# Narrow pieces of the output product in triples instead of pairs, on one core

## The chip, the cores and the metric

The kernel runs on one core of a Trainium2 chip. Its time is the device time of one launch in microseconds, the median of several runs. It computes with five engines: TensorE (PE, with its weight loads as PEld), VectorE (DVE), ScalarE (ACT), GpSimd (POOL) and SyncE (SP), which issues the DMAs.

## What is computed

Attention over chunks of 32 rows with some context and memory rows, then two feed-forward blocks on its 3072 rows of 512 columns. The change lies in the last one:

```python
x = attention(q, k, v, mem_k, mem_v)              # 3072 x 512
h = x @ moe_w_in                                  # 512 x 2048
x = (relu(h) + log1p(exp(-abs(h)))) @ moe_w_out
out = ((x @ moe2_w_a) * (x @ moe2_w_b)) @ moe2_w_out    # 512 x 1536, 1536 x 512
```

## The kernel before

Every float is split into a high and a low fp32r part, and a product is made of three matmuls: high x high, high x low, low x high. The stage of the change is the last block. Its 3072 tokens are worked in `NPAIR` = 3 pairs of two blocks of 512 tokens, and in each pair over `NF2` = 12 steps f of 128 of the 1536 inner columns. A step computes a and b of both token blocks by seven wide products of Winograd's kind instead of eight (`product`, L808, six matmuls of 512 columns each, recorded at L815): 11, s2, s3, s1, 12, 22, s4, in that order, into the PSUM tiles pX, pY, pW, pV, pX, pW, pV. VectorE adds them up behind each (`tt`, L949 to L991) into q and r, which are the products a*b of the two token blocks.

Two steps, even and odd, are a group m (`GROUP` = 2). In the second and third pair, all groups but the very last (11 in all) are worked by `block_step` (L936), and their output product too is of Winograd's kind: from q and r of both steps the operands a11, s3 (even step) and s1, s2, a22, a12, s4 (odd step) are made by VectorE and GpSimd, split by ScalarE (`hi_of`, recorded at L921) and VectorE or GpSimd (`lo_of`, L925). A product of them with the weights `w2o` and `tw` is done in 14 pieces in the next group's two steps, in the order `TURNS` (L867). A piece is called by its product and half here:

1.0 1.1 5.0 6.0 6.1 3.0 7.0 7.1 5.1 4.0 4.1 3.1 2.0 2.1

A piece (`block_product`, L872) is six narrow matmuls of 256 columns (L888) into a PSUM bank, and an addition of the bank to the output tile y by VectorE (L899; a copy by ScalarE, L897, where it is the first). Products 1, 6, 7, 4 and 2 use bank `acc1` for half 0 and `acc2` for half 1; 5 and 3 use `acc3`. Each bank exists once, so a piece waits until the addition of the piece before it on that bank has read it. In a pair's last group the finished y is stored from there (L902).

Where the pieces stand is said by `next_blocks(f, k)` (L909), called seven times a step, behind each wide product: k = 0 behind 11, 1 behind s2, 2 behind s3, 3 behind s1, 4 behind 12, 5 behind 22, 6 behind s4. In the code of a step this is

```python
        at(5)
        next_job()
        next_blocks(f, 5)
        if odd:
            ...                                   # s1 (L983), s2 (L986), their high halves
        product(v, p, f, "s4", False)
        tt(q, v, q, ALU.add)                      # L990
        tt(q, x, q, ALU.mult)                     # L991
        if odd:
            lo_of(p, m, "s1", s1, V)
            lo_of(p, m, "s2", s2, G)
            ...
        at(6)
        next_blocks(f, 6)
```

All engines work in the order in which the program issues (`manual_schedule`, L1190). `at(k)` (L1244) issues the fetches of the weights of the next step (`fetch_u` L800, `fetch_o` L804, `fetch_t` L796), and in step 11 of the second pair and step 0 of the third the splits of the third pair's operands (`split_hi`, `split_lo`, L665). The last group of the third pair is worked by `pair_step` (L1013), which calls `next_blocks` in the same places; in its odd step one piece stands at k = 5 and none at k = 6, and the last one comes behind all steps (L1325).

Of the kernel before, what the change touches and what calls it, by code (L numbers as in the profile page):

```python
# [47 lines left out]
GROUP = 2  # L48
# [3 lines left out]
def attn_moe_moe2(ctx: ExitStack, tc: tile.TileContext, q, k, v, mem_k, mem_v,  # L52
# [851 lines left out]
    def next_job(blocks=False):  # L904
        if jobs and (len(jobs[0]) == 5) == blocks:
            p, m, *which = jobs.pop(0)[:4]
            (block_product if blocks else job)(p, m, *which)

    def next_blocks(f, k):  # L909
        if (f + k) % GROUP == 0:  # L910
            next_job(True)
            next_job(True)

    due = {}
# [21 lines left out]
    def block_step(p, f, at):  # L936
# [6 lines left out]
        nc.scalar.copy(q, x)  # L943
        at(0)
        next_blocks(f, 0)
        late_due(0)
        y = bank("att", f"pY{p}_{f}")
# [5 lines left out]
        at(1)  # L953
        next_job()
        next_blocks(f, 1)
        w = bank("att", f"pW{p}_{f}")
        product(w, p, f, "s3", True)
        r = temp("r", f"r{p}_{f}")
        tt(r, w, q, ALU.add)
        at(2)  # L960
        next_job()
        next_blocks(f, 2)
        late_due(2)
        v = bank("acc0", f"pV{p}_{f}")
# [403 lines left out]
```

## Time and profile before

| | |
|---|---|
| median of 3 runs | 1160.2 us (1159.97 to 1160.5) |
| the profiled execution | 1160.61 us, of which the span of instructions 1158.8 |
| TensorE (PE) busy | 1149.9 us, 99% of the span |
| weight loads (PEld) | 1009.2 us, 87% |
| VectorE (DVE) | 820.7 us, 71% |
| ScalarE (ACT) | 542.0 us, 47% |
| GpSimd (POOL) | 354.3 us, 31% |

How to read it: shares are of the whole span, so they mix stages. An engine off the path may be busy or idle at no cost; what counts is what the bounding engine stands for. Names such as pz (narrow pieces), pX to pV (wide products), y, gh, e, d, s, o_s, o_a are the program's tiles.

### The profile page before, as it was taken

To read this page: it belongs to the slowest core of one execution; us is meant where nothing else is said; L and a number is where in the kernel's file an instruction comes from. 1 tells how busy PE (TensorE), PEld (TensorE's weight loads), DVE (VectorE), ACT (ScalarE), POOL (GpSimd) and SP (SyncE) were. 2 spreads that over 40 slices of the span, in tenths; PEclk is the share of its full clock that TensorE was granted. 3 is DMA by queue.
4 is the path that set the end of the run, shared out by engine and by line. 5 is a ranking of instruction groups with operands and counts; after the bars stand their busy time and mean duration, and the time that the engine had idled before them with its cause. 6 is when DMAs were issued, how large, how long until landed. Compare 5 with 4: busy or idle time off the path is not lost.

```text
span 1158.8 us, 20590 instructions
## 1 busy us (share of the span) xinstructions
PE 1149.9 (99%) x7474; PEld 1009.2 (87%) x7474; DVE 820.7 (71%) x1700; ACT 542.0 (47%) x1233; POOL 354.3 (31%) x296
## 2 busy tenths in 40 slices
PE   9999999999999999999999999999999999999998
PEld 7899999999998888888888888888888888888887
DVE  6889668767677657652376777988667779667776
ACT  6899666665665665554654433232321123221120
POOL 2000323232232223222313565811323544323330
PEclk9999999999999999999999999999999999999999
DMA  8964264454454353321734668672975553975521
GB/s 226 274 227 101 68 142 125 119 132 97 101 130 115 80 132 103 96 68 56 236 134 165 255 254 311 251 273 104 364 273 203 182 200 110 342 279 197 198 84 73
DMA packets 199061, 199.32 MB, mean 172 GB/s; under 512 B 123648, under 2 KB 152240, under 8 KB 198960
## 3 DMA queue, kind: packets, MB, share of 16 engines
q1 hardware_dynamic: 198576, 197.96, 53.6%
q8 instruction: 59, 0.97, 0.3%
q14 instruction: 42, 0.34, 0.1%
q0 software_dynamic: 384, 0.05, 0.0%
HBM read 141.33 MB, written 56.62 MB: 171 GB/s over the span
## 4 chain that ended last, share of the span: by engine, by line
PE 91%; ACT 3%; DVE 3%; DMA 1%; issue 1%; SPq 1%; DVEq 0%; ACTq 0%
PE px L594 21%; PE ph L561 21%; PE pz L888 10%; PE pW L815 9%; PE pV L815 8%; PE pX L815 8%; PE py L850 6%; PE pY L815 4%; PE pxa L482 2%; PE sc L437 1%; DMA kp<-in_k_dram 1%; DVE tmp L126 1%; ACT sm L387 1%; DVE w L134 0%; ACT work L387 0%
## 5 line engine op out<-in xcount | busy, mean ns | idle before, releaser
L561 PE MATMUL ph<-x,w 128*128 128x384 f32 (+1 forms) x1344 | 285.4, 360 | 0.1
L594 PE MATMUL px<-gh,w 128*128 128x384 f32 (+1 forms) x896 | 266.8, 358 | 0.0
L561 PEld LDWEIGHTS ph<-x,w 128*128 128x128 f32 x1344 | 240.6, 188 | 24.8 <-ACT x L373 0.2
L573 DVE SCALAR_TENSOR_TENSOR e<-ph,e 128x384 f32<-128x384 f32 (+1 forms) x112 | 68.7, 614 | 161.0 <-ACT e L572 160.5
L594 PEld LDWEIGHTS px<-gh,w 128*128 128x128 f32 x896 | 165.5, 188 | 15.7 <-DVE e L607 0.3
L594 PE MATMUL px<-gl,w 128*128 128x384 f32 (+1 forms) x448 | 160.3, 358 | 0.0
L582 POOL TENSOR_TENSOR gl<-e,gh 128x384 fp32r<-128x384 f32 (+1 forms) x80 | 94.9, 1187 | 178.9 <-ACT gh L579 178.8
L899 DVE TENSOR_TENSOR y<-pz,y 128x512 f32<-128x512 f32 x138 | 91.1, 683 | 17.6 <-PE pz L888 14.7
L570 ACT ACTIVATE e<-ph 128x384 f32<-128x384 f32 (+1 forms) x112 | 59.5, 531 | 90.4 <-PE ph L561 71.6
L579 ACT CAST gh<-e 128x384 fp32r<-128x384 f32 (+1 forms) x112 | 62.6, 559 | 79.4 <-DVE e L573 59.8
L594 PEld LDWEIGHTS px<-gl,w 128*128 128x128 f32 x448 | 84.1, 188 | 7.6
L925 POOL TENSOR_TENSOR o_s<-s,o_s 128x512 fp32r<-128x512 f32 x33 | 43.4, 1314 | 147.0 <-ACT o_s L921 144.5
L921 ACT CAST o_s<-s 128x512 fp32r<-128x512 f32 x44 | 27.4, 622 | 125.3 <-DVE s L983 92.6
L850 PE MATMUL py<-w2o,c 128*128 128x512 f32 (+1 forms) x342 | 84.8, 386 | 0.1
L454 DVE STREAM_TRANSPOSE af<-sm 32x256 f32<-32x256 f32 x180 | 78.2, 434 | 2.6
L850 PEld LDWEIGHTS py<-w2o,c 128*128 128x128 f32 x342 | 63.4, 188 | 13.9 <-DVE c L1070 0.8
L387 ACT ACTIVATE sm<-sm,st 128x96 f32<-128x96 f32 x168 | 60.6, 362 | 19.2 <-DVE st L383 19.2
L572 ACT ACTIVATE e<-e 128x384 f32<-128x384 f32 (+1 forms) x112 | 64.0, 571 | 3.5
L571 ACT ACTIVATE e<-e 128x384 f32<-128x384 f32 (+1 forms) x112 | 64.0, 571 | 3.5
L921 ACT CAST o_a<-e 128x512 fp32r<-128x512 f32 x22 | 13.7, 621 | 96.6 <-DVE e L991 81.6
L394 POOL TENSOR_TENSOR sm<-sm,st 128x768 f32<-128x768 f32 x18 | 26.5, 1473 | 103.2 <-DVE st L392 103.2
L888 PEld LDWEIGHTS pz<-tw,o_s 128*128 128x128 f32 x396 | 53.4, 190 | 3.7
(191 smaller groups left out, 2130.4 us busy)
## 6 DMA issues: line engine op xcount, KB each, us to landing
u<-u_scratch SPq DMA_DIRECT2D x72, 512.0 KB
u_scratch<-u SPq DMA_DIRECT2D x36, 512.0 KB
w2o<-w2o_scratch SPq DMA_DIRECT2D x24, 512.0 KB
tw<-t_scratch SPq DMA_DIRECT2D x22, 512.0 KB
raw<-in_moe_w_in_dram SPq DMA_DIRECT2D x16, 512.0 KB
raw<-in_moe_w_out_dram SPq DMA_DIRECT2D x16, 512.0 KB
vn<-in_v_dram SPq DMA_DIRECT2D x35, 176.0 KB
raw_a<-in_moe_w_a_dram SPq DMA_DIRECT2D x12, 512.0 KB
```

The lines of the kernel that those rows point to most:

```text
L387: nc.scalar.activation(sm[:, h], sm[:, h], AF.Exp, bias=st[:, 0, h:h + 1], scale=-1.0, accum_out=st[:, 1, h:h + 1])
L454: nc.vector.transpose(out=af[32 * kb:32 * kb + 32, x], in_=self.sm[32 * x:32 * x + 32, :, 32 * kb:32 * kb + 32])
L561: nc.tensor.matmul(ph, lhsT=w[:, a, kt * P:(kt + 1) * P], rhs=x[:, c, kt, :], start=n == 0, stop=n == 3 * KT - 1)
L571: nc.scalar.activation(e, e, AF.Exp, scale=-1.0)
L572: nc.scalar.activation(e, e, AF.Ln, bias=1.0)
L573: nc.vector.scalar_tensor_tensor(e, ph, 0.0, e, ALU.max, ALU.add)
L582: engine.tensor_tensor(lo, e, hi.bitcast(F32), ALU.subtract)
L594: nc.tensor.matmul(acc[t][i][:, :WIDTHS[t]], lhsT=a, rhs=c, start=f == 0 and m == 0, stop=f == NF1 - 1 and m == 2)
L815: nc.tensor.matmul(bank[:, :T2], lhsT=u[:, j, a, kt * P:kt * P + P], rhs=x[kt][:, c], start=first_ and m == 0, stop=m == 3 * KH - 1, skip_ ...
L850: nc.tensor.matmul(b, lhsT=c[:, x, r], rhs=w[:, y, cols], start=n == 0, stop=n == 3 * GROUP - 1)
L888: nc.tensor.matmul(b[:, j], lhsT=c[:, x, r], rhs=w(y), start=begin and i == j == 0, stop=i == 2, skip_group_check=True)
L899: tt(y, b, y, ALU.add)
```

## The change

`next_blocks` no longer issues two pieces wherever f + k is even, but a number given by a table over the step's parity and k. The order of the pieces stays.

```diff
     def next_blocks(f, k):
-        if (f + k) % GROUP == 0:
-            next_job(True)
+        for _ in range({(0, 1): 3, (0, 4): 3, (1, 0): 3, (1, 3): 3, (1, 6): 2}.get((f % GROUP, k), 0)):
             next_job(True)
```

Before, the pairs stand at k = 0, 2, 4, 6 of the even step and 1, 3, 5 of the odd one: seven places a group. After it, triples stand at k = 1 and 4 of the even and 0 and 3 of the odd step, and a pair (2.0, 2.1) at k = 6 of the odd one: five places.

## Rows read from the trace of the kernel before

**Rows 1.** The page, part 1: busy us (share of the span) and instructions of each engine

```profile
PE 1149.9 (99%) x7474; PEld 1009.2 (87%) x7474; DVE 820.7 (71%) x1700; ACT 542.0 (47%) x1233; POOL 354.3 (31%) x296
```

**Rows 2.** Busy time by stretches: us, busy of each engine, granted clock, DMA share, GB/s

```profile
968.00:998.00 30.00, 29.83 (x166) 25.29 (x165) 26.54 (x37) 7.14 (x11) 12.94 (x8) 1.00 0.41 130
```

**Rows 3.** Timeline of TensorE: start us, us, engine, line, out<-in, count

```profile
905.63 1.59 PE L888 MATMUL pz<-w2o,o_a 128*128 128x256 f32 x12
907.06 1.55 PE L815 MATMUL pV<-xb,u 128*128 128x512 f32 x6
908.45 1.52 PE L815 MATMUL pX<-x,u 128*128 128x512 f32 x6
909.81 1.59 PE L888 MATMUL pz<-w2o,o_a 128*128 128x256 f32 x12
```

**Rows 4.** Timeline of VectorE, the end of an odd step

```profile
905.83 0.69 DVE L975 TENSOR_TENSOR d<-pW,e 128x512 f32<-128x512 f32 x1 [2.06 <-PE pW L815]
906.56 0.69 DVE L976 TENSOR_TENSOR gh<-d,gh 128x512 f32<-128x512 f32 x1
907.17 1.28 DVE L899 TENSOR_TENSOR y<-pz,y 128x512 f32<-128x512 f32 x2
908.37 0.68 DVE L983 TENSOR_TENSOR s<-gh 128x512 f32<-128x512 f32 x1
909.15 0.69 DVE L986 TENSOR_TENSOR s<-s,e 128x512 f32<-128x512 f32 x1
909.76 0.68 DVE L990 TENSOR_TENSOR e<-pV,e 128x512 f32<-128x512 f32 x1
...
911.09 1.33 DVE L925 TENSOR_TENSOR o_s<-s,o_s 128x512 fp32r<-128x512 f32 x1
912.34 1.27 DVE L899 TENSOR_TENSOR y<-pz,y 128x512 f32<-128x512 f32 x2
```

**Rows 5.** Waits from 815 us on: waiter, releaser, us in total, times, longest

```profile
PEld pz L888 <- DVE y L899: 0.4, 1, 0.4
```

**Rows 6.** Timelines of TensorE and VectorE, where the second pair ends

```profile
967.10 1.52 PE L815 MATMUL pX<-x,u 128*128 128x512 f32 x6
968.56 1.69 PE L888 MATMUL pz<-w2o,o_a 128*128 128x256 f32 x12
970.09 1.55 PE L815 MATMUL pY<-xs,u 128*128 128x512 f32 x6
...
967.82 1.28 DVE L899 TENSOR_TENSOR y<-pz,y 128x512 f32<-128x512 f32 x2
```

**Rows 7.** The chain of waits (start, us, what), and splits in VectorE's timeline

```profile
964.31 1.57 PE pz L888 x12
...
973.00 1.77 PE pz L888 x12
...
976.16 1.36 PE pX L815 x6
979.62 1.39 PE pW L815 x6
981.01 1.63 PE pV L815 x6
...
957.27 2.31 DVE L665 TENSOR_TENSOR x<-x,x 128x1024 fp32r<-128x1024 f32 x1
...
966.69 1.22 DVE L665 TENSOR_TENSOR xa<-xs,xa 128x1024 fp32r<-128x1024 f32 x1
```

**Rows 8.** Timelines of GpSimd and VectorE: the subtractions of low halves

```profile
910.58 1.29 POOL L925 TENSOR_TENSOR o_s<-s,o_s 128x512 fp32r<-128x512 f32 x1 [11.91 <-ACT o_s L921]
...
956.67 0.68 DVE L925 TENSOR_TENSOR o_a<-e,o_a 128x512 fp32r<-128x512 f32 x1
```

**Rows 9.** Timelines of SyncE's queue and TensorE, first group of the third pair

```profile
999.37 0.39 SPq L806 DMA_DIRECT2D w2o<-w2o_scratch  x1
...
1008.27 0.88 PE L888 MATMUL pz<-w2o,o_s 128*128 128x256 f32 x6
```

## The prediction

> **What bounds the kernel now.** The page comes first: TensorE is busy for 1149.9 us, 99% of the span [rows 1], so time comes from TensorE being given less work, packing it closer, or standing still. The table by stretches then shows the stage of the change: TensorE has 29.83 of 30.00 us busy even where one pair of token blocks gives way to the next, at a granted clock of 1.00, the 2.4 GHz level [rows 2]. The timeline of TensorE shows how pieces follow each other (below), and the list of waits says how often a piece has stood for an addition of VectorE: once, 0.4 us [rows 5]. So before the change additions come in time almost everywhere, and the question is whether they still do. VectorE's timeline answers that [rows 4].
>
> The profiled execution took 1160.61 us for its span of 1158.8; the median of the runs is 1160.2. I work out a difference in that profile and set it on the median; the 0.4 us between them doesn't matter.
>
> **Part 1: fewer changes between wide and narrow.** Both kernels issue the same 14 pieces a group and 11 groups. Timed from start to start [rows 3]: a pair of pieces takes 1.43 us (905.63 to 907.06), the wide product behind it 1.39 (907.06 to 908.45), a wide product behind a wide one 1.36 (908.45 to 909.81). A change back to wide thus costs 0.03 us. A group has seven now and five afterwards: 2 x 0.03 x 11 = 0.7 us. The rows are rounded to 0.01, so it lies between 0.4 and 0.7; I take **-0.5 us**. A row of a triple is missing; by the pair's pace it takes 2.15. This price has no cover to lose: TensorE is the bound. The work itself (matmuls, additions, stores) is the same, and costs nothing extra.
>
> **Part 2: the last pair of a group moves behind the end of the odd step.** Before, 2.0 and 2.1 stand at k = 5, and VectorE adds them at 907.17, right behind the two operations on r (905.83, 906.56) and ahead of s1, s2, the two on q and the low half of s1 [rows 4]. After, they stand at k = 6: their additions come behind all of these in VectorE's order, which is the program's. Who waits for them: pieces 1.0 and 1.1 of the next group, which write the same PSUM banks (`acc1`, `acc2`). TensorE's way from 2.1 to 1.0 stays two wide products, s4 and 11 before, 11 and s2 after.
>
> Let d be the start of the addition behind product 22 (L975); it comes 0.20 us after that product's successor starts (905.83 against 905.63 [rows 3, 4]).
> - VectorE. d to s1 is 2.54 us, of which the two additions 1.20 (907.17 to 908.37). Without them s1, which reads what L976 just wrote, starts 0.73 behind it, as L976 does behind d: d + 1.46. From s1 to the low half of s1 are 2.72 us (908.37 to 911.09), from there to the next operation 1.25 (912.34): 2.0's addition starts at d + 5.43. It takes 0.68 (L983 and L990 are of that size; two additions together 1.28), so bank `acc1` is free at **d + 6.11**. Nothing else sets these times: product s4 ends on TensorE at d + 1.2, piece 2.0 at d + 1.9, both long before VectorE turns to them.
> - TensorE. s4 starts at d - 0.20, then s4 1.36 (now behind a wide one), the pair 1.43, product 11 1.39, product s2 1.36: piece 1.0 is due at **d + 5.34**.
>
> It is late by 0.77 us. What lateness costs is shown once already, where the additions were delayed by other work: product 12 before it starts at 967.10, so the pair is due at 968.46, and the product behind it at 969.89; bank `acc1` was free at 967.82 + 0.68 = 968.50, 0.04 late, and the product behind started at 970.09, 0.20 late [rows 6]. So a late bank costs its lateness and 0.16 more (the wait, and a first matmul whose weights could not be loaded ahead). Each such place costs 0.77 + 0.16 = 0.93. The addition of 2.1 ends 0.61 behind 2.0's, while 1.1 is due 0.72 behind 1.0: no second wait.
>
> How often: at the even steps 4, 6, 8, 10 of the second pair, and 2, 4, 6, 8, 10 of the third (2 follows the second pair's last group): nine, **+8.4 us**. The start of the second pair has no pieces ahead of it.
>
> **Part 3: the turn from the second to the third pair.** There VectorE's list also holds splits of the next pair's operands (L665), one of them between L976 and s1: 966.69, 1.13 us to the next operation at 967.82 [rows 6, 7]. If VectorE reaches L975 on time, 2.0's bank is late by 0.77 + 1.13, which costs 2.06 with the 0.16. Another split, at k = 1, takes 2.31 us now (957.27 [rows 7]); in the new order three additions stand ahead of it, GpSimd's subtraction beside it stays in its place, and it may take 1.2 as the one at 966.69 does. If it does not, L975 is up to 1.1 late, and the wait is 3.2. I take 2.1, as most splits are short. In exchange the waits of now can go, since TensorE comes later and finds its operands ready. The chain of waits shows them as pairs over 1.43 or products over 1.39: 0.14 at 964.31, 0.20 at 968.56 [rows 6], 0.34 at 973.00, 0.67 between 976.16 + 1.36 and 979.62 (a pair stands there, of which 1.43 is its due), 0.27 at 981.01 (against 1.36); 1.6 in all. 2.1 - 1.6 = **+0.5**, between -1.6 (no wait left) and +3.2 (all of them stay).
>
> **Part 4: the other pieces.** 5.0 is the only other one that comes earlier (k = 2 to k = 1). Its low half of s1 ends at d + 5.5 and it is due past d + 7.5. All others come at the same place or later, so operands have more time. Banks: 6.x, 7.x, 4.x each follow the reading of their predecessor by three wide products, 4.1 us, and three additions end 0.9 us after the third piece. VectorE's d waits for TensorE, so three additions at k = 3 are over before it. No cost, range 0 to 0.1 a group.
>
> The queue of SyncE: no DMA is added; in the first two steps of the third pair, output stores wait on it for the additions, fetches behind them. The last two move from about d + 2.6 to d + 6.7. The fetch of w2o behind them went out at 999.37, 8.9 us ahead of its piece at 1008.27 [rows 9]; by my sums it goes out 5.7 ahead. No row gives its landing; it can cost between 0 and the lost 3.2 us, once. I take 0, since the store and fetches queued ahead of it then find an emptier queue. Elsewhere no store stands between the fetches.
>
> Sum: -0.5 + 8.4 + 0.5 = +8.4; 1160.2 + 8.4 = **1168.6 us**.
>
> **A rule against the row.** The low half of s1 takes 1.33 us on VectorE in every group [rows 4]; GpSimd runs its own subtraction from 910.58 to 911.87, begun 0.51 us before it [rows 8]. The same operation (L925) took 0.68 at 956.67 [rows 8], before GpSimd had begun one. I take 1.25, as in the row, since GpSimd's start hangs on s2, and both keep their distance to it. The Trainium skill, "SBUF — State Buffer", section "Who interferes with whom", says that whichever of the two issues first holds the shared port pair, and the other is blocked. The rows agree; by that rule the sum hangs on this order, which is the second rival.
>
> **The rivals.**
> 1. *The bank is free in time, no slower.* This would need VectorE to take the additions of 2.x as soon as their matmuls are done (d + 2), not in the program's order, or its list to be 0.8 us shorter between d and 2.0. For it: only one wait of this kind now [rows 5]. Against: VectorE starts nothing out of the order written in rows 4. It decides at d + 5.34. Then part 1 alone is left: 1159.7; with the waits of part 3 gone too, 1158.1. Chance 0.10; even the second is not over 0.2% faster, and takes something more that I don't see (0.03 of the 0.10).
> 2. *VectorE's low half of s1 gets ahead of GpSimd's.* 0.65 us shorter: lateness 0.12, 0.28 a place, 9 x 0.28 = 2.5, and part 3 at about -0.1: 1160.2 + 2.5 - 0.1 - 0.5 = 1162.1. It needs s2's high half on ScalarE to come half a microsecond later. Chance 0.05.
> 3. *TensorE's clock falls.* Ten waits at a regular distance. After waits of 0.67 and 0.27 us in the stretch 968 to 998 the granted clock stays at 1.00 [rows 2, 7]. Should one wide product after each wait run at 1.2 GHz, that is 1.36 us more ten times: 1182.2. Chance 0.03. The Trainium skill, "TensorE: Matmul & The Clock Gate", section "A second HAM failure mode: psum-queue depth-cycling", tells of a kernel whose short idle times between groups made the clock go back and forth; no row here shows that.
> 4. *The fetch is late too* (part 4): up to 1171.8. Counted with the forecast.
>
> **How the numbers follow.** The forecast with its fetch has 0.82. Its own bounds: a place costs 0.77 (its lateness alone) to 1.09 (the 0.16 twice), nine of them 6.9 to 9.8; part 3 at -1.6 to +3.2, fetch 0 to 3.2, part 1 at -0.7 to -0.4. All low ends together give 1164.8; all high ends, 1176.0, hardly meet. As the range I give 1164.5 to 1172.5, in which some 0.8 of the chance lies. Rivals 1, 2 and 3 lie outside it (0.18). A measurement of this kernel can tell about 0.2%, 2.3 us, from no change. Slower by more than that, over 1162.5: the forecast and rival 3, 0.85, and a part of rival 2, 0.02; within: the rest of rivals 1 and 2, 0.10; faster: 0.03.
>
> **What would show it.** In the profile afterwards: in the list of waits, weight loads of pz for y (L899), about ten, 7 to 11 us in all; in the timeline of TensorE, a pause ahead of each pz behind pY in an even step; triples at 2.15 us; in VectorE's timeline, two L899 behind L925 at the odd step's end, starting 5.4 us behind L975. Wrong would be: no such waits, VectorE taking 2.x ahead of s1, the low half of s1 at 0.7 us, or TensorE standing for a DMA or at a lower granted clock.

## The result, and the profile after

The changed kernel takes 1169.58 us (median of 6 runs, 1168.74 to 1170.31), the kernel before 1160.24 (6 runs): 1.0079 times as long, with a 95% interval of 1.0069 to 1.0089. It is 9.3 us slower; the forecast was 8.4.

Lines behind 909 are one lower in the changed kernel: L974 is L975 of before, L924 is L925, and so on. The list of waits from 815 us on (waiter, releaser, us in total, times, longest) has what [rows 5] did not:

```profile
PEld pz L888 <- DVE y L899: 12.0, 10, 2.1
PE pz L888 <- DMA w2o<-w2o_scratch: 1.1, 1, 1.1
```

Ten pieces stand for an addition. The 12.0 us are idle time of the weight loads, counted from the end of the load before, which lies ahead of the moment at which the piece is due; the lateness of the ten pieces themselves is 9.3 us (0.83 nine times and 1.87, below). The last line is a wait for a fetch. The table by stretches (columns as in [rows 2]) shows TensorE idle for 0.67 us of an ordinary group and 1.71 where the pairs turn, at a granted clock of 1.00 in both:

```profile
878.00:908.00 30.00, 29.33 (x170) 25.59 (x169) 21.95 (x32) 5.21 (x9) 8.97 (x7) 1.00 0.58 198
966.00:997.00 31.00, 29.29 (x169) 25.59 (x168) 26.72 (x37) 8.63 (x13) 13.71 (x8) 1.00 0.44 153
```

One place in the timeline of TensorE, to be set beside [rows 3]:

```profile
907.75 1.60 PE L888 MATMUL pz<-w2o,o_a 128*128 128x256 f32 x12
909.19 1.55 PE L815 MATMUL pX<-x,u 128*128 128x512 f32 x6
910.57 1.52 PE L815 MATMUL pY<-xs,u 128*128 128x512 f32 x6
912.76 1.69 PE L888 MATMUL pz<-w2o,o_a 128*128 128x256 f32 x12 [0.67 <-DVE y L899]
914.29 0.88 PE L888 MATMUL pz<-tw,o_s 128*128 128x256 f32 x6
915.01 1.55 PE L815 MATMUL pW<-xs,u 128*128 128x512 f32 x6
```

The pair 2.0, 2.1 stands behind s4 (907.75), and then 1.0 starts 2.19 us behind the start of s2 instead of 1.36: 0.83 late. The triple takes 2.25 from 912.76 to 915.01, where one without a wait takes 2.15 (a row is in experiment 1): together 0.93. VectorE in the same stretch, beside [rows 4]:

```profile
906.59 0.69 DVE L974 TENSOR_TENSOR d<-pW,e 128x512 f32<-128x512 f32 x1 [2.06 <-PE pW L815]
...
910.78 1.33 DVE L924 TENSOR_TENSOR o_s<-s,o_s 128x512 fp32r<-128x512 f32 x1
912.03 1.27 DVE L899 TENSOR_TENSOR y<-pz,y 128x512 f32<-128x512 f32 x2
```

It never pauses from d (906.59) on. 2.0's addition begins 5.44 us behind d and ends 0.68 later, at 912.71; piece 1.0 starts at 912.76.

At the turn of the pairs one split stands ahead of all this, and the wait is 1.71 (columns of the timelines):

```profile
970.86 1.52 PE L815 MATMUL pY<-xs,u 128*128 128x512 f32 x6
974.09 1.70 PE L888 MATMUL pz<-w2o,o_a 128*128 128x256 f32 x12 [1.71 <-DVE y L899]
...
966.94 0.68 DVE L974 TENSOR_TENSOR d<-pW,e 128x512 f32<-128x512 f32 x1
...
968.26 1.22 DVE L665 TENSOR_TENSOR xa<-xs,xa 128x1024 fp32r<-128x1024 f32 x1
...
973.36 1.27 DVE L899 TENSOR_TENSOR y<-pz,y 128x512 f32<-128x512 f32 x2
```

The fetch, beside [rows 9], in the timelines of SyncE's queue and of TensorE:

```profile
1004.22 0.97 SPq L902 DMA_DIRECT2D out_dram<-y  x2
...
1006.31 0.41 SPq L806 DMA_DIRECT2D w2o<-w2o_scratch  x1
...
1010.61 1.59 PE L888 MATMUL pz<-tw,o_s 128*128 128x256 f32 x12
1013.26 0.95 PE L888 MATMUL pz<-w2o,o_s 128*128 128x256 f32 x6 [1.05 <-DMA w2o<-w2o_scratch]
```

Piece 3.0 is due at 1010.61 + 1.43 = 1012.04, and 1.2 late. The fetch went out 5.7 us ahead of that.

**The sum closes.** From the start of product 11 in step 2 of the second pair to the start of the last matmul of L815, TensorE needs 322.52 us before (820.67 to 1143.19) and 332.11 after (819.69 to 1151.80): 9.59 more. Nine places of 0.93 make 8.37; the turn costs 1.98 (1.87 and a first matmul), where 1.6 of waits are gone [rows 6, 7]; the fetch 1.28; fewer changes between wide and narrow give 0.4 back. 8.37 + 1.98 - 1.6 + 1.28 - 0.4 = 9.6. The spans differ by 8.6 only, as the stage began 1 us sooner in this execution than in that of before; over all the traces here it begins between 819.6 and 821.1, whatever the edit.

### The profile page after: what moved, and what is told of

It is laid out like the page before. It is cut to its first block, busy times and chain, and to the rows that moved or that the text cites. A ratio compares the mean times of both kernels' runs of the same rounds, so it can differ in the third digit from the quotient of the medians.

```text
span 1167.4 us, 20615 instructions
## 1 busy us (share of the span) xinstructions
PE 1150.6 (99%) x7474; PEld 1008.4 (86%) x7474; DVE 820.7 (70%) x1700; ACT 541.6 (46%) x1233; POOL 354.4 (30%) x296
## 4 chain that ended last, share of the span: by engine, by line
PE 90%; DVE 6%; ACT 2%; DMA 1%; issue 1%; POOL 0%; DVEq 0%; ACTq 0%; POOLq 0%
PE ph L561 23%; PE px L594 22%; PE pz L888 8%; PE pW L815 8%; PE pV L815 7%; PE pX L815 7%; PE py L850 6%; PE pY L815 3%; PE pxa L482 2%; PE sc L437 1%; DVE o_s L924 1%; DMA w2o<-w2o_scratch 1%; DVE y L899 1%; PE ptk L290 1%; DVE gh L975 1%
## 5 line engine op out<-in xcount | busy, mean ns | idle before, releaser
L899 DVE TENSOR_TENSOR y<-pz,y 128x512 f32<-128x512 f32 x138 | 93.5, 687 | 31.0 <-PE pz L888 24.4
L924 POOL TENSOR_TENSOR o_s<-s,o_s 128x512 fp32r<-128x512 f32 x33 | 43.1, 1305 | 138.1 <-ACT o_s L920 124.1
L815 PE MATMUL pW<-xs,u 128*128 128x512 f32 x216 | 55.2, 391 | 0.0
```

The source lines that it names most:

```text
L815: nc.tensor.matmul(bank[:, :T2], lhsT=u[:, j, a, kt * P:kt * P + P], rhs=x[kt][:, c], start=first_ and m == 0, stop=m == 3 * KH - 1, skip_ ...
L899: tt(y, b, y, ALU.add)
```

## The experiments

The theory: 2.0 and 2.1 stand behind the odd step's end, their additions come behind all of VectorE's work there, and the next pieces on their banks wait. The rival that the result itself leaves open: triples mean three additions in a row, which make VectorE late. Each kernel is the changed one with the edit shown, unless another is named, and is compared with the kernel before.

**1. The last pair back, the triples kept.**

```diff
-        ... (1, 3): 3, (1, 6): 2}
+        ... (1, 3): 3, (1, 5): 2}
```

> The four triples stay, only the last pair goes back to k = 5. If the place of 2.0 and 2.1 behind the odd step's end makes the waits (the theory), all ten waits of pz for y are gone, and so is the wait of 3.0 for its fetch at the start of the third pair: between 1158.3 and 1160.2 us. If three additions of VectorE in a row make the banks late (the rival), at least four of five places still have them, and it stays above 1167.

Measured: 1158.98 us, 0.9989 of before (interval 0.9980 to 0.9997). All ten waits for y and the wait for the fetch are gone, and the 44 triples bring none of their own. The rival falls. One of the nine places (1.0 starts 1.36 behind s2, and the triple takes 2.15), and then the one wait that is left, within the triple at the turn:

```profile
909.79 1.52 PE L815 MATMUL pY<-xs,u 128*128 128x512 f32 x6
911.15 1.59 PE L888 MATMUL pz<-w2o,o_a 128*128 128x256 f32 x12
...
913.30 1.55 PE L815 MATMUL pW<-xs,u 128*128 128x512 f32 x6
...
971.02 0.40 PE L888 MATMUL pz<-tw,o_s 128*128 128x256 f32 x2
972.06 0.74 PE L888 MATMUL pz<-tw,o_s 128*128 128x256 f32 x4 [0.65 <-DVE o_s L924]
```

Piece 5.0 has done its first two matmuls, with the high half of s1, and stands for the low one. This is the one version whose interval lies below 1, by little: it ends at 0.9997. The medians differ by 1.3 us.

**2. The last pair late, without triples.**

```diff
+        ... {(0, 0): 2, (0, 2): 2, (0, 4): 2, (0, 6): 2, (1, 1): 2, (1, 3): 2, (1, 6): 2}
```

> Pairs at all places of before, only the last pair moved from k = 5 to k = 6; no triple anywhere. By the theory 1.0 is due one wide product (1.36 us) sooner than in the changed kernel, so each of nine places costs 0.77 + 1.36 + 0.16 = 2.29 us, 20.6 in all, and the turn of the pairs some 1.8 more than before: about 1182. By the rival (triples) there is nothing left to wait for: 1159 to 1161.

Measured: 1192.43 us, 1.0274 (1.0260 to 1.0288). No triple, and the largest loss of all; each of the nine places waits 2.16 us and 0.10 in its first matmul, 2.26 where 2.29 were expected:

```profile
882.56 1.55 PE L815 MATMUL pX<-x,u 128*128 128x512 f32 x6
886.11 1.69 PE L888 MATMUL pz<-w2o,o_a 128*128 128x256 f32 x12 [2.00 <-DVE y L899]
887.64 1.55 PE L815 MATMUL pY<-xs,u 128*128 128x512 f32 x6
```

(886.11 - 882.56 = 3.55, where 1.39 is due, as product 11 stands behind a pair here.) But 10 us more were lost than expected, and the expectation missed them. Behind other such waits TensorE is slow for a while. Timeline, and table by stretches:

```profile
853.01 1.99 PE L888 MATMUL pz<-w2o,o_a 128*128 128x256 f32 x12 [2.00 <-DVE y L899]
854.80 2.76 PE L815 MATMUL pY<-xs,u 128*128 128x512 f32 x6
857.36 1.67 PE L815 MATMUL pW<-xs,u 128*128 128x512 f32 x6
...
854.00:857.50 3.50, 3.50 (x13) 2.92 (x13) 1.38 (x2) 0.37 (x1) 3.06 (x3) 0.53 0.00 1
```

Product s2 takes 2.56 us here (854.80 to 857.36) instead of 1.39, with the granted clock at 0.53 in this stretch, nearly all of it at the 1.2 GHz level. Before it fell, TensorE had stood for 2.2 us. The pair, s2 and s3 together lose 1.6 us. The trace has six such stretches in this run, 9.3 us in all, which with 20.3 at the nine places and 2.7 more at the turn is 32.3; the medians differ by 32.1.

**3. One operation of VectorE moved behind the two additions.**

```diff
-            lo_of(p, m, "s1", s1, V)
...
         next_blocks(f, 6)
         if odd:
+            lo_of(p, m, "s1", s1, V)
```

> The changed kernel with one operation moved in VectorE's order: the low half of s1 behind the two additions of 2.0 and 2.1. Bank acc1 is then free 1.25 us sooner, at 4.86 us behind L975 where piece 1.0 is due at 5.34: by the theory the waits at nine places are gone, while piece 5.0 finds its operand just in time (0 to 0.2 us a place): 1160 to 1163, the fetch's wait of some 1 to 2 us left. By the rival it stays above 1167.

Measured: 1160.73 us, 1.0002 (0.9993 to 1.0011). TensorE issues what it does in the changed kernel; only VectorE's order differs, and the nine waits are gone. VectorE, then TensorE:

```profile
908.86 1.28 DVE L899 TENSOR_TENSOR y<-pz,y 128x512 f32<-128x512 f32 x2
910.06 0.68 DVE L924 TENSOR_TENSOR o_s<-s,o_s 128x512 fp32r<-128x512 f32 x1
...
908.66 1.52 PE L815 MATMUL pY<-xs,u 128*128 128x512 f32 x6
910.02 1.59 PE L888 MATMUL pz<-w2o,o_a 128*128 128x256 f32 x12
```

The bank is free at 909.54, 0.48 ahead of piece 1.0, and the low half takes 0.68; GpSimd's subtraction is over by then (it ends at 909.65). Left are waits at the turn (0.6 and 1.2) and the fetch's (0.9).

**4. The first triple one product later.**

```diff
-        ... {(0, 1): 3, ...
+        ... {(0, 2): 3, ...
```

> The changed kernel with the first triple at k = 2 of the even step instead of k = 1, all else as it is, the pair still at k = 6. Piece 1.0 is due one wide product later, 6.70 us behind L975, and the bank is free at 6.11: by the theory no wait at the nine places, a short one (0.5 to 0.7) at the turn of the pairs, and the fetch's wait at the start of the third pair left (1.3 to 2.2): 1159 to 1162. By the rival above 1167.

Measured: 1160.71 us, 1.0003 (0.9993 to 1.0012). No wait at the nine places, 0.5 at the turn, as expected. The fetch's wait is 1.9 (1008.06, where 1004.70 + 1.43 = 1006.13 is due), and behind it the clock falls, as in experiment 2: product 22 takes 2.57 us (1008.96 to 1011.53).

```profile
1004.70 1.59 PE L888 MATMUL pz<-tw,o_s 128*128 128x256 f32 x12
1008.06 1.11 PE L888 MATMUL pz<-w2o,o_s 128*128 128x256 f32 x6 [1.77 <-DMA w2o<-w2o_scratch]
1008.96 2.77 PE L815 MATMUL pW<-xb,u 128*128 128x512 f32 x6
1011.53 1.82 PE L815 MATMUL pV<-xb,u 128*128 128x512 f32 x6
```

The execution shown, 1161.9 us, and one other, 1162.82, have a mean granted clock of 0.998; the other eight, with 0.999 or 1.000, took 1159.77 to 1160.89. So the fall does not seem to come every time.

**5. GpSimd's subtraction behind VectorE's.**

```diff
-            hi_of(p, m, "s2", s2)
...
-            lo_of(p, m, "s2", s2, G)
...
             hi_of(p, m, "a12", q)
+            hi_of(p, m, "s2", s2)
+            lo_of(p, m, "s2", s2, G)
```

> The changed kernel with the high half of s2 (ScalarE) moved behind that of a12, so that GpSimd's subtraction begins behind VectorE's low half of s1. If GpSimd's operation beside it is what makes that take 1.33 us, it takes 0.68 now, the bank is 0.12 us late instead of 0.77 and a place costs 0.28 instead of 0.93: 5.9 us less at nine places and 0.65 less at the turn, about 1163. If the 1.33 has another cause, it stays at 1169 to 1170.

Measured: 1167.31 us, 1.0057 (1.0041 to 1.0072). At the nine places it is as expected: the low half of s1 takes 0.68 with GpSimd starting behind it, and 1.0 comes 1.54 behind s2's start, 0.18 late.

```profile
910.91 0.68 DVE L924 TENSOR_TENSOR o_s<-s,o_s 128x512 fp32r<-128x512 f32 x1
...
912.30 1.29 POOL L924 TENSOR_TENSOR o_s<-s,o_s 128x512 fp32r<-128x512 f32 x1 [13.28 <-PE pY L815]
...
910.71 1.52 PE L815 MATMUL pY<-xs,u 128*128 128x512 f32 x6
912.25 1.69 PE L888 MATMUL pz<-w2o,o_a 128*128 128x256 f32 x12
```

The time missed the expected 1163, through the turn, where the edit puts GpSimd's split of 1024 columns ahead of its subtraction and beside VectorE's multiplication into r (L975 in this kernel, L976 before):

```profile
966.45 2.40 POOL L665 TENSOR_TENSOR xa<-x,xa 128x1024 fp32r<-128x1024 f32 x1 [7.86 <-ACT xa L658]
...
966.50 2.90 DVE L975 TENSOR_TENSOR gh<-d,gh 128x512 f32<-128x512 f32 x1
```

An operation of 0.69 takes 2.90, the bank comes 3.4 us late, and the clock falls behind that pause too.

**6. Two stores behind the fetch.** The stores of the second pair's 2.0 and 2.1 are kept in a list and issued behind `next_blocks(f, 1)` of the next step.

```diff
-            nc.sync.dma_start(out[...]..., y)
+            store = partial(nc.sync.dma_start, out[...]..., y)
+            held.append(store) if n == "2" else store()
...
         next_blocks(f, 1)
+        while held:
+            held.pop(0)()
         w = bank("att", f"pW{p}_{f}")
```

> The changed kernel with the second pair's last output stores (2.0 and 2.1) issued behind the fetches of w2o and tw of the next step instead of ahead of them. If those stores hold up the fetch of w2o for which piece 3.0 stands 1.3 us at the start of the third pair, that wait is gone and nothing else changes: about 1168.3, the ten waits for y as they are. If the DMA queues are too full there anyway, it stays at 1169.6 with the wait.

Measured: 1169.09 us, 1.0076 (1.0063 to 1.0090). The fetch goes out at 999.49, its piece follows without a wait, and the ten waits for y are as in the changed kernel:

```profile
999.49 0.38 SPq L806 DMA_DIRECT2D w2o<-w2o_scratch  x1
...
1011.59 1.59 PE L888 MATMUL pz<-tw,o_s 128*128 128x256 f32 x12
1013.02 0.88 PE L888 MATMUL pz<-w2o,o_s 128*128 128x256 f32 x6
```

The stage is 1.3 us shorter than in the changed kernel (330.81 against 332.11); of that the medians show 0.5, within what they scatter. So the cause of this wait is shown in the trace, its price in the time only roughly.

**7. The pair back, and a split at the turn moved from k = 5 to k = 6** (experiment 1 with L665's split of s1's operand behind the low half of s1).

> The kernel with the pair back at k = 5, and at the turn of the pairs one split of the next pair's operands (low half of s1's operand, 1.2 us on VectorE) moved from k = 5 to k = 6, behind the low half of s1 of the output product. The one wait of 0.9 us left there (5.0 for that low half) should go: about 1158.0, ahead of both kernels. If the wait has another cause it stays at 1159.0.

Measured: 1159.72 us, 0.9996 (0.9987 to 1.0005). This is not the 1158.0 expected: 5.0 no longer stands, but product s1 of the third pair now does, for the split that was moved:

```profile
972.81 0.39 PE L815 MATMUL pV<-xa,u 128*128 128x512 f32 x1
973.96 1.43 PE L815 MATMUL pV<-xa,u 128*128 128x512 f32 x5 [0.77 <-DVE xa L665]
```

**8. Pairs, the last late, and the low half of s1 behind it** (experiments 2 and 3 together).

> Pairs only, the last at k = 6 (as in the second experiment), with the low half of s1 behind the two additions (as in the third). A place's lateness falls from 2.13 to 0.87 us, so it costs 1.03 instead of 2.29: nine of them 9.3, the turn about 1 more than before. If the clock fell in the second experiment because the single pauses there were 2.2 us and longer, it stays at 1.00 here, and the time is 1169 to 1172. If ten pauses of any length bring it down, 1175 or more.

Measured: 1173.19 us, 1.0107 (1.0093 to 1.0121), between the two expectations. The nine places cost 0.94 and 0.11, near the 1.03 expected, and behind none of them does TensorE slow down (912.17 - 909.84 is 2.33 instead of 1.39, and the pair behind it takes 1.54):

```profile
909.84 1.55 PE L815 MATMUL pX<-x,u 128*128 128x512 f32 x6
912.17 1.70 PE L888 MATMUL pz<-w2o,o_a 128*128 128x256 f32 x12 [0.78 <-DVE y L899]
913.71 1.55 PE L815 MATMUL pY<-xs,u 128*128 128x512 f32 x6
```

At the turn the pause is 3.0 us, and behind it the granted clock is 0.51 (from 974 to 981, nearly all at the 1.2 GHz level), which costs 2.9 us in this trace. The one execution of the four whose mean granted clock is 1.000 took 1170.78, inside the first expectation. So it was not the number of pauses.

**9. Both moves: the pair at k = 5, the first triple at k = 2.**

> Both moves together: the last pair at k = 5 of the odd step and the first triple at k = 2 of the even step. The one wait left with the pair back alone (0.9 us, piece 5.0 at the turn of the pairs) should go, as 5.0 comes one wide product (1.36 us) later; the nine places stay without a wait, and the fetch of w2o goes out as early as before. By the theory 1157.7 to 1158.6, ahead of both kernels. If the waits only depend on how many additions stand together, it is no better than 1159.

Measured: 1159.62 us, 0.9994 (0.9985 to 1.0004). 5.0 no longer waits, but at the turn piece 6.0 does, 1.44 us: it now follows 1.0 on its bank by two wide products instead of three, and 1.0's addition stands behind a split of 2.35 us.

```profile
976.63 1.69 PE L888 MATMUL pz<-tw,o_s 128*128 128x256 f32 x12 [1.28 <-DVE y L899]
...
973.63 2.35 DVE L665 TENSOR_TENSOR xb<-x,xb 128x1024 fp32r<-128x1024 f32 x1
975.90 1.87 DVE L899 TENSOR_TENSOR y<-pz,y 128x512 f32<-128x512 f32 x3
```

In experiments 7 and 9 a wait that is moved away comes back at a later place, again for VectorE. So the turn seems to be bound by VectorE's list there; no run shortens that list.

## Why the prediction was right

**Part 1**, fewer changes: -0.5 forecast; triples take 2.15 us and a product behind one 1.39, so -0.4. Alone it can't be told from no change; experiment 1 has it and some of the waits at the turn gone, 1.3 us together.

**Part 2**, the nine places: +8.4 forecast, 8.4 in the trace. d to 2.0's addition: 5.43 forecast, 5.44 measured; lateness with its 0.16: 0.93 and 0.93. (The product that starts at 967.10 in the prediction's price of a late bank is 11, not 12; its sum stays the same.) Experiments 1, 3 and 4 take the wait away in three ways that each leave the triples in place (the pair sooner, VectorE's order, the next piece later), and 2 and 8 change its size with the distance on TensorE and on VectorE: 2.26 and 1.05 against 2.29 and 1.03 by the same sum. So this part is shown.

**Part 3**, the turn: 2.06 forecast, 1.98 measured, and the 1.6 of old waits went. That VectorE would reach L975 about on time was a choice between two bounds, and it was the right one: it starts at 966.94, 0.26 behind s4, as the split at k = 1 took 1.22 us (at 960.54) instead of 2.31, for the reason given there.

**Part 4**, the fetch: the distance of 5.7 us was right, the price of 0 wrong. It cost 1.28, inside its bounds of 0 to 3.2. The step that failed is that 5.7 us would be enough because the queue would be emptier: from its issue to the start of its piece the fetch took 6.95 us (1006.31 to 1013.26), and 6.97 and 6.72 in experiments 3 and 4, where two stores and two fetches go out right ahead of it too. Sent out 13.5 us ahead of the piece and before the two stores, it is in time (experiment 6). TensorE standing for a DMA was named as a sign of being wrong, and it came, once. With this term the sum would have been 1169.9.

**The rivals.** The first (bank free in time) did not come; experiments 1, 3 and 4 show what it would have been, 1159 to 1161. The second is real as a mechanism: experiment 5 has its 0.68 and a wait of 0.28 in all. The Trainium skill, "SBUF — State Buffer", section "Who interferes with whom", says that the order of issue decides which of the two is blocked; the 1.33 with GpSimd ahead agrees. The 0.68 of experiments 3 and 5 does not test it, as the two operations do not overlap there. The third did not come in the changed kernel, whose longest pause was 1.9 us, but did in experiments 2, 4, 5 and 8. What the Trainium skill, "TensorE: Matmul & The Clock Gate", section "A second HAM failure mode: psum-queue depth-cycling", tells of a clock that goes back and forth is seen in experiment 2, with six falls.

## What to carry to other kernels

A piece that reuses a bank is bound to the place of its predecessor's evacuation in the evacuating engine's order, not to that of its matmuls: when pieces are moved, count the engine's work from the last thing that it must wait for (here L975) to that evacuation, and set it against the time on TensorE to the next user. Where such work can follow the evacuation instead of standing ahead of it, one moved line takes the nine waits away as moving the pieces does (experiment 3), though other waits stayed: 1160.73 us against 1158.98 in experiment 1. Grouping narrow pieces in threes costs nothing by itself; the version with the lowest median here keeps the triples and leaves the last pair at k = 5.

## What was not expected of the hardware

- Behind a pause TensorE may go on at the 1.2 GHz level for some products, at a price of about 1.6 us each time in experiment 2 and 2.9 in experiment 8. In the traces it did so behind single pauses of 1.9 us (experiment 4), 3.0 (8), 3.4 (5) and 4.2 (the turn in 2), and behind five of the nine pauses of 2.2 in experiment 2. It did not behind the other four there, as at 886.11, where product s2 behind the pair has its usual 1.39 us, nor behind the pause of 1.9 us at the turn of the changed kernel (and of experiment 6), nor behind any of 0.8 to 1.4. What tells pauses of the same length apart stays open.
- VectorE's operations with both inputs in SBUF grow when GpSimd works beside them, by about what GpSimd has left: 0.68 to 1.33 beside 1.29, 0.69 to 2.90 beside 2.40.
- A matmul that stood for a semaphore is followed by the next one up to 0.1 us later than in a stream (2.25 against 2.15 for the triple), so each wait costs some more than its own length.
